# Retention and SwiGLU kernel: the last two units' rows and transposes of chunk 3 three steps later, and one down piece split in two

## The chip, the cores and the metric

The kernel runs on one core of a Trainium2 chip. The metric is the device time in microseconds of one execution, given as the median of several runs. One execution was profiled, and all times within it are in microseconds from the start of its span.

## The reference

q, k and v have the shape (4 batches, 8 heads, 768 positions, 64). Each head has a decay gamma. The output is then normalized and run through a feed-forward layer with 512 inputs and 1536 inner columns:

```
for t in range(S):
    state = gamma * state + outer(k[t], v[t])       # per batch and head, 64 x 64
    y[t]  = scale * q[t] @ state
x   = y, with the heads side by side                # 3072 rows of 512
xn  = x / sqrt(mean(x * x) + 1e-06) * rms_g
out = (silu(xn @ w_gate) * (xn @ w_val)) @ w_out
```

## The kernel before

**Tiling.** The 768 positions are cut into six chunks of 128 (chunks 0 to 5). A unit (c, b) is chunk c of batch b; a pair (c, p) is two batches. Within a chunk the recurrence is done as products: q times k (the "q-k products", `ap` for chunks 0 and 1, `a_pe` from chunk 2 on), a causal mask on VectorE, then the masked products times v, plus q times the state that the earlier chunks left (`values`). The pair's result is scaled (`y_out`), squared on ScalarE (`square`), its norm factor is made on GpSimd (`rstd`), and VectorE writes the normalized rows (`norm`).

**Operands.** For chunks 2 to 5, `load` (L105) issues three transfers per unit on GpSimd's DMA queue: q and k, converted to bf16, and v in float32. `t_dma` (L472) then issues two DMA transposes per unit on SP's queue, to have q and k with the head dimension on the partitions. `x_dma` (L541) does the same for the normalized rows. SP's queue also issues the output stores (`store`, L569), which for chunks 0 and 1 are two half transfers per unit. An instruction on a queue waits until those ahead of it have been issued. A DMA also waits for the eighth one before it on its kind of queue to have landed, since eight semaphores take turns.

**Feed-forward.** A group is the four units of one chunk, 512 rows. `gv` (L548) computes gate and value products into PSUM, ScalarE applies silu, VectorE multiplies, and the result lies in hT. `down` (L576) multiplies one unit's hT by w_out in 12 accumulating matmuls, ScalarE copies the result to SBUF, and SP stores it. The last half unit of the kernel uses `down_last`.

**Order.** Everything is in an order written out by hand, with one instruction stream per engine. Up to the first group's down pieces it is a straight list (L596 to L737). After it, `run` goes through a list of steps for each chunk: 12 `gv` steps and four `down` steps for chunk 1, twelve `gv` steps (four of 256 rows, eight of 512) and four `down` steps for later chunks. After each step a table names what else is issued. So while the feed-forward group of chunk 1 runs, chunk 2's attention and chunk 3's loads and transposes are put between its steps. Chunk 3's first q-k products (units 0 and 1) follow step 12 of chunk 1; its second (units 2 and 3) follow step 5 of chunk 2.

**PSUM.** Eight banks. In the straight list a bank is taken from the head of a written list (`first`, then `order`), so the order of the calls decides the bank. From chunk 1's steps on, the attention and the feed-forward turn in four banks each. The output rows o_sb have three buffers; the raw q and k rows and their transposes have eight each, v has six.

Of the kernel before, what the change touches and what calls it, by code (L numbers as in the profile page):

```python
# [16 lines left out]
def kernel(  # L17
# [21 lines left out]
    NFF = DFF // 128  # L39
# [25 lines left out]
    def bank(name, dtype=F32, ffn=False, i=None):  # L65
        if i is None and split[0]:
            i = turn[ffn] % 4 + 4 * ffn
            turn[ffn] += 1
        elif i is None and first:
            i = first.pop(0)  # L70
        elif i is None:
            i = order[0]
            order.append(order.pop(0))
        return psum.tile([128, 512 if dtype == F32 else 1024], dtype, name=name, tag=f"p{i}")
# [30 lines left out]
    def load(c, b, names="qkv"):  # L105
        u = U.setdefault((c, b), {})
        for n in names:
            if n == "v":
                x = work.tile([128, H, D], F32, name="v_f", tag="v_f", bufs=6)
                nc.gpsimd.dma_start(out=x, in_=unit_v[n][c, b])  # L110
            else:
                x = work.tile([128, DM], BF16, name=n + "b", bufs=8)
                nc.gpsimd.dma_start(out=x.rearrange("p (h d) -> p h d", h=H), in_=unit_v[n][c, b])  # L113
            u[n] = x
# [106 lines left out]
    def copy(eng, out, in_):  # L221
        return (nc.scalar.copy if eng == "a" else nc.vector.tensor_copy)(out, in_)  # L222
# [44 lines left out]
    def ap(c, p, a):  # L267
        u = U[c, p]
        if c == 0:
            qt, kt = ([u[n + "T", a][:, :, b] for b in range(2)] for n in "qk")  # L270
        else:
            qt, kt = u["qT", a], u["kT", a]
        ps = [bank("a_ps") for _ in range(2)]
        for x in range(2):
            for e in range(2):
                o = (x * 2 + e) * 128
                for b in range(2):
                    for i in range(2):
                        r, t = slice(i * 64, i * 64 + 64), slice(b * 64, b * 64 + 64)
                        nc.tensor.matmul(ps[i][t, o:o + 128], kt[b][r, x, e], qt[b][r, x], start=True, stop=True)  # L280
        u["a_ps", a] = ps
# [104 lines left out]
    def x_pe(c, p, j):  # L386
        u = U[c, p]
        ps = bank("x_ps", BF16)
        for s in range(KS):
            nc.tensor.transpose(ps[:, s * 128:(s + 1) * 128], u["xn"][j][:, s * 128:(s + 1) * 128], ident)  # L390
        u["x_ps", j] = ps

    def x_copy(c, p, j, eng):
        b = 2 * p + j
        dst = XT[c][:, :, b * C:(b + 1) * C]
        src = U[c, p]["x_ps", j][:, :512].rearrange("p (s t) -> p s t", s=KS)
        if c == 0 and j == 0:
            nc.vector.tensor_tensor(out=dst, in0=src, in1=g_col[:, :, None].to_broadcast([128, KS, 128]), op=ALU.mult)
        else:
            return copy(eng, dst, src)  # L400
# [71 lines left out]
    def t_dma(c, b):  # L472
        u = U[c, b]
        for n in "qk":
            t = work.tile([128, NHP, 128], BF16, name=n + "T", tag=n + "T", bufs=8)
            nc.sync.dma_start_transpose(out=t, in_=u[n])
            u[n + "T"] = t
# [91 lines left out]
    def store(eng, c, b, m, o_sb):  # L569
        if c < 2:  # L570
            for e in range(2):
                eng.dma_start(out=out_e[c, b, e][:, m], in_=o_sb[e * 64:e * 64 + 64, m])
        else:
            eng.dma_start(out=out_v[c, b][:, m], in_=o_sb[:, m])

    def down(c, b):  # L576
        ps = bank("o_ps", ffn=True)
        for n in range(NFF):
            nc.tensor.matmul(ps, HT[c][:, n, b * C:(b + 1) * C], wo_b[:, n, :], start=n == 0, stop=n == NFF - 1)  # L579
        o_sb = work.tile([128, DM], F32, name="o_sb", bufs=3)  # L580
        nc.scalar.copy(o_sb, ps)  # L581
        store(nc.sync, c, b, slice(0, DM), o_sb)
# [125 lines left out]
    load(2, 0)  # L708
    y1(0)
    down(0, 0)  # L710
    y1_out(0)
    square(1, 0, 0)
# [5 lines left out]
    vp_pair(1, 1)  # L718
    load(2, 2)
    down(0, 1)  # L720
    down(0, 2)
    t_dma(2, 0)
    for n, e in (("q", "a"), ("k", "v")):
        tp1(1, n)
        tc1(1, n, e)
# [1 line left out]
    x_copy(1, 0, 0, "v")  # L727
    x_pe(1, 0, 1)
    x_copy(1, 0, 1, "v")
    ap(1, 1, 0)  # L730
    ap(1, 1, 1)
    for a in range(2):
# [1 line left out]
            ap_mask(1, 1, a, i)  # L734
    load(2, 3)
    t_dma(2, 1)
    down(0, 3)  # L737

    def run(steps, after):
        for i, step in enumerate(steps):  # L740
# [4 lines left out]
    def L(f, *a):  # L745
        return lambda: f(*a)
# [13 lines left out]
        5: [L(a_pair, 2, 0), L(a_mask, 2, 0, 0)],  # L760
        6: [L(a_mask, 2, 0, 1), L(a_mask, 2, 1, 0), L(vp, 2, 2), L(vp, 2, 3)],
        7: [L(a_mask, 2, 1, 1)],
        8: [L(values, 2, 0), L(y_out, 2, 0, 0), L(y_out, 2, 0, 1), L(state_add, 2, 0), L(load, 3, 2),
            L(t_dma, 3, 0), L(t_dma, 3, 1)],
        9: [L(square, 2, 0, 0), L(load, 3, 3)],
        10: [L(a_pair, 2, 1), L(square, 2, 0, 1), L(a_mask, 2, 2, 0), L(a_mask, 2, 2, 1), L(state_cast, 0),
             L(rstd, 2, 0)],
        11: [L(a_mask, 2, 3, 0), L(a_mask, 2, 3, 1), L(t_dma, 3, 2)],
        12: [L(values, 2, 1, (3, 0), True), L(norm, 2, 0, 0, 1), L(x_dma, 2, 0, 0), L(x_dma, 2, 0, 1),
             L(y_out, 2, 1, 0), L(y_out, 2, 1, 1), L(square, 2, 1, 0), L(square, 2, 1, 1), L(rstd, 2, 1),  # L770
             L(state_add, 2, 1), L(a_mask, 3, 0, 0), L(a_mask, 3, 0, 1), L(norm, 2, 1, 0, 1),
             L(x_dma, 2, 1, 0), L(x_dma, 2, 1, 1), L(t_dma, 3, 3), L(a_mask, 3, 1, 0, 1),
             L(state_cast, 1), L(vp, 3, 0), L(vp, 3, 1)],
    })

    for c in range(2, NCH):
# [64 lines left out]
```

## Time and profile before

| | us |
|---|---|
| median of 8 runs | 239.39 |
| lowest and highest run | 236.74 and 243.71 |
| profiled execution, whole | 240.19 |
| its span from first to last instruction | 238.4 |
| TensorE busy in the span | 226.4 |
| VectorE, GpSimd, ScalarE busy | 127.2, 114.9, 87.5 |

The feed-forward group of chunk 1 starts at 62.00 us with its first gate product, and that of chunk 2 at 100.46. The last matmul is that of `down_last`, which starts at 232.50.

In a timeline row the first number is the start and the second the time; x counts the instructions merged in it, and a bracket gives the idle time of the engine before it and what ended it. A row with SPq or POOL and a DMA operation is the issue of a transfer, not the transfer; its landing comes later. In the list of waits the three numbers are total time, count and longest. In the chain, a DMA piece runs from a transfer's issue to its landing.

### The profile page before, as it was taken

Reading aid. Unit: us, or ns where it says so; the run is one execution under the profiler, and the core shown is the slowest. Engines: PE = TensorE matmul, PEld = TensorE weight load, DVE = VectorE, ACT = ScalarE, POOL = GpSimd, SP = SyncE. Lnnn points to the kernel's source line nnn. Section 1 sums busy time; section 2 is a strip of 40 time slices with the busy share of each in tenths; the row PEclk is TensorE's granted clock in tenths of the full one; section 3 lists DMA queues with packets and bytes.
Section 4 is the critical chain, followed back from the end, with each engine's and each line's share of the span. In section 5 each row is a group of like instructions: output and inputs, shape, how many; then the busy total and the mean of one; then the engine's idle time right before and its main releaser. Section 6 shows DMA issues by size and latency. Waiting matters only on the chain.

```text
span 238.4 us, 5562 instructions
## 1 busy us (share of the span) xinstructions
PE 226.4 (95%) x2290; PEld 138.7 (58%) x2290; DVE 127.2 (53%) x222; ACT 87.5 (37%) x176; POOL 114.9 (48%) x150
## 2 busy tenths in 40 slices
PE   7786899989999998999999999999999999999994
PEld 2355685545788875585454585454684544864443
DVE  3675634735576877627868036868145842234300
ACT  2863644323143333235324235323235342333211
POOL 8957499749959951980946802937001001000000
PEclk9999999999999999999999999999999999999999
DMA  7999999999999999699990999991630204200022
GB/s 95 167 174 210 157 158 171 202 198 189 180 156 194 174 173 181 73 148 246 96 171 5 194 174 204 98 124 36 166 110 0 47 0 132 91 0 0 0 92 88
DMA packets 83307, 30.25 MB, mean 127 GB/s; under 512 B 69521, under 2 KB 78993, under 8 KB 83282
## 3 DMA queue, kind: packets, MB, share of 16 engines
q0 software_dynamic: 51328, 16.52, 69.3%
q1 hardware_dynamic: 31280, 13.25, 28.5%
q8 instruction: 18, 0.29, 0.5%
q10 hardware_dynamic: 674, 0.14, 0.3%
q14 instruction: 7, 0.06, 0.1%
HBM read 28.32 MB, written 6.29 MB: 145 GB/s over the span
## 4 chain that ended last, share of the span: by engine, by line
PE 73%; DMA 18%; POOL 3%; DVE 2%; ACT 1%; issue 1%; DVEq 0%; SPq 0%; ACTq 0%; POOLq 0%
PE o_ps L579 23%; PE g_ps L560 21%; PE v_ps L560 21%; DMA v2f<-in_v_dram 7%; DMA wo_b<-in_moe_w_out_dram 5%; DMA kT<-kb 4%; DMA k2b<-in_k_dram 2%; PE a_ps L485 1%; PE y_ps L514 1%; PE o_ps L590 1%; PE y_ps L531 1%; POOL q2b L101 1%; POOL k2b L101 1%; POOL vp L300 1%; PE kv_ps L523 1%
## 5 line engine op out<-in xcount | busy, mean ns | idle before, releaser
L565 DVE TENSOR_TENSOR hT<-sg,v_ps 128x512 bf16<-128x512 bf16 (+1 forms) x76 | 49.8, 658 | 77.3 <-PE v_ps L560 65.4
L560 PE MATMUL v_ps<-xnT,wv_b 128*128 128x256 bf16 (+1 forms) x428 | 74.9, 309 | 1.8 <-DMA wv_b<-in_moe_w_val_dram 1.8
L560 PE MATMUL g_ps<-xnT,wg_b 128*128 128x256 bf16 (+1 forms) x428 | 75.1, 310 | 0.2 <-ACT xnT L222 0.2
L564 ACT ACTIVATE sg<-g_ps 128x512 bf16<-128x512 f32 (+1 forms) x76 | 43.5, 575 | 75.2 <-PE g_ps L560 75.2
L579 PE MATMUL o_ps<-wo_b,hT 128*128 128x512 bf16 x276 | 61.1, 379 | 0.9 <-DMA wo_b<-in_moe_w_out_dram 0.9
L560 PEld LDWEIGHTS <-wv_b 128*128 128x128 bf16 x428 | 41.8, 98 | 22.7 <-DMA wv_b<-in_moe_w_val_dram 2.0
L560 PEld LDWEIGHTS <-wg_b 128*128 128x128 bf16 x428 | 40.6, 98 | 20.6 <-issue 0.7
L579 PEld LDWEIGHTS <-hT 128*128 128x128 bf16 x276 | 26.6, 98 | 32.7 <-issue 1.2
L454 POOL TENSOR_SCALAR m<-ms 128x2 f32<-128x2 f32 x10 | 2.2, 218 | 68.6 <-ACT xsq L449 68.5
L581 ACT COPY o_sb<-o_ps 128x512 f32<-128x512 f32 x23 | 13.4, 584 | 46.5 <-PE o_ps L579 43.5
L462 DVE SCALAR_TENSOR_TENSOR xn<-x,rstd,g_bc 128x512 bf16<-128x512 f32 x20 | 19.5, 1004 | 10.4 <-POOL rstd L370 10.4
L494 DVE TENSOR_TENSOR am<-a_ps,causal 128x512 bf16<-128x512 f32 x32 | 21.1, 681 | 0.0
L468 POOL TENSOR_TENSOR vp<-v_f,vd_n 128x512 bf16<-128x512 f32 x16 | 19.4, 1238 | 0.0
L113 POOL DMA_DIRECT2D qb<-in_q_dram x16 | 15.1, 944 | 1.8 <-DMA wo_b<-in_moe_w_out_dram 1.8
L449 ACT ACTIVATE xsq<-x 128x512 bf16<-128x512 f32 x20 | 12.4, 623 | 9.3 <-DVE x L440 9.3
L113 POOL DMA_DIRECT2D kb<-in_k_dram x16 | 14.4, 898 | 1.8 <-DMA wo_b<-in_moe_w_out_dram 1.8
L110 POOL DMA_DIRECT2D v_f<-in_v_dram x16 | 14.7, 921 | 0.1
L440 DVE TENSOR_TENSOR x<-y_ps,yd_n 128x512 f32<-128x512 f32 x16 | 10.6, 685 | 1.7 <-PE y_ps L531 1.7
L219 PE MATMUL hot<-ones 128*128 128x512 bf16 x28 | 9.4, 466 | 1.4 <-DVE ones L146 1.4
L300 POOL TENSOR_TENSOR vp<-v2f,vd_p 128x1024 bf16<-128x1024 f32 x4 | 7.7, 1930 | 0.1
L370 POOL TENSOR_TENSOR rstd<-m,mhalf 128x2 f32<-128x2 f32 x10 | 7.2, 718 | 0.8
L101 POOL DMA_DIRECT2D q2b<-in_q_dram x8 | 5.8, 738 | 0.8 <-POOLq L825 0.8
(96 smaller groups left out, 154.4 us busy)
## 6 DMA issues: line engine op xcount, KB each, us to landing
v_f<-in_v_dram POOLq DMA_DIRECT2D x16, 256.0 KB, 6.6
out_dram<-o_sb SPq DMA_DIRECT2D x15, 256.0 KB, 2.3
out_dram<-o_sb SPq DMA_DIRECT2D x17, 128.0 KB, 6.0
qb<-in_q_dram POOLq DMA_DIRECT2D x16, 128.0 KB, 5.6
kb<-in_k_dram POOLq DMA_DIRECT2D x16, 128.0 KB, 6.3
wg_b<-in_moe_w_gate_dram POOLq DMA_DIRECT2D x6, 256.0 KB, 8.2
wv_b<-in_moe_w_val_dram POOLq DMA_DIRECT2D x6, 256.0 KB, 9.0
wo_b<-in_moe_w_out_dram POOLq DMA_DIRECT2D x3, 512.0 KB, 10.9
```

The costliest lines, as they stand in the source:

```text
L110: nc.gpsimd.dma_start(out=x, in_=unit_v[n][c, b])
L113: nc.gpsimd.dma_start(out=x.rearrange("p (h d) -> p h d", h=H), in_=unit_v[n][c, b])
L440: nc.vector.tensor_tensor(out=x[:, :, :, i, :], in0=u["y"][i].rearrange("p (b a d) -> p b a d", b=2, a=NHP), in1=yd_n[:, c, i][:, None, :, ...
L449: nc.scalar.activation(xsq, u["x"][:, b], AF.Square, scale=1.0 / math.sqrt(DM), accum_out=u["ms_"][:, b:b + 1])
L462: nc.vector.scalar_tensor_tensor(out=u["xn"][b], in0=u["x"][:, b], scalar=u["rstd"][:, b:b + 1], in1=g_bc, op0=ALU.mult, op1=ALU.mult)
L468: nc.gpsimd.tensor_tensor(out=x, in0=U[c, b]["v"], in1=vd_n[:, c, :, None].to_broadcast([128, H, D]), op=ALU.mult)
L494: nc.vector.tensor_tensor(out=x, in0=u["a_ps"][i].rearrange("p (a t) -> p a t", a=NHP), in1=causal[:, None, :].to_broadcast([128, NHP, 128 ...
L560: nc.tensor.matmul(x[:, o:o + w], wt[:, s, n * 128:(n + 1) * 128], XT[c][:, s, t0:t1], start=s == 0, stop=s == KS - 1)
L564: nc.scalar.activation(sg[:, :m], ps[0][:, :m], AF.Silu)
L565: return nc.vector.tensor_tensor(out=HT[c][:, n0:n1, t0:t1], in0=sg[:, :m].rearrange("p (n t) -> p n t", t=w), in1=ps[1][:, :m].rearrange( ...
L579: nc.tensor.matmul(ps, HT[c][:, n, b * C:(b + 1) * C], wo_b[:, n, :], start=n == 0, stop=n == NFF - 1)
L581: nc.scalar.copy(o_sb, ps)
```

## The change

Three things move; no work is added or taken away.

`down` can now do a part of its 12 matmuls, and keeps its PSUM bank between the parts. The down piece of unit (0, 3) is cut: four of its matmuls now come ahead of chunk 1's second q-k products, and eight stay where all 12 were.

The transposes of unit (2, 0) are issued ahead of the down piece and the store of unit (0, 2), and not behind them.

The loads of chunk 3's units 2 and 3 move from after steps 8 and 9 of chunk 1 to after step 11 and into step 12, where they stand ahead of the second pair's scaling. Their transposes move from after step 11 and the end of step 12 to after steps 14 and 15.

```diff
-    def down(c, b):
-        ps = bank("o_ps", ffn=True)
-        for n in range(NFF):
+    DP = {}
+
+    def down(c, b, n0=0, n1=NFF):
+        ps = DP[b] = bank("o_ps", ffn=True) if n0 == 0 else DP[b]
+        for n in range(n0, n1):
             nc.tensor.matmul(ps, HT[c][:, n, b * C:(b + 1) * C], wo_b[:, n, :], start=n == 0, stop=n == NFF - 1)
+        if n1 < NFF:
+            return
         o_sb = work.tile([128, DM], F32, name="o_sb", bufs=3)
...
     down(0, 1)
+    t_dma(2, 0)
     down(0, 2)
-    t_dma(2, 0)
...
     x_copy(1, 0, 1, "v")
+    down(0, 3, 0, 4)
     ap(1, 1, 0)
     ap(1, 1, 1)
...
     t_dma(2, 1)
-    down(0, 3)
+    down(0, 3, 4)
...
-        8: [L(values, 2, 0), L(y_out, 2, 0, 0), L(y_out, 2, 0, 1), L(state_add, 2, 0), L(load, 3, 2),
+        8: [L(values, 2, 0), L(y_out, 2, 0, 0), L(y_out, 2, 0, 1), L(state_add, 2, 0),
             L(t_dma, 3, 0), L(t_dma, 3, 1)],
-        9: [L(square, 2, 0, 0), L(load, 3, 3)],
+        9: [L(square, 2, 0, 0)],
...
-        11: [L(a_mask, 2, 3, 0), L(a_mask, 2, 3, 1), L(t_dma, 3, 2)],
+        11: [L(a_mask, 2, 3, 0), L(a_mask, 2, 3, 1), L(load, 3, 2)],
         12: [L(values, 2, 1, (3, 0), True), L(norm, 2, 0, 0, 1), L(x_dma, 2, 0, 0), L(x_dma, 2, 0, 1),
+             L(load, 3, 3),
              L(y_out, 2, 1, 0), L(y_out, 2, 1, 1), L(square, 2, 1, 0), L(square, 2, 1, 1), L(rstd, 2, 1),
              L(state_add, 2, 1), L(a_mask, 3, 0, 0), L(a_mask, 3, 0, 1), L(norm, 2, 1, 0, 1),
-             L(x_dma, 2, 1, 0), L(x_dma, 2, 1, 1), L(t_dma, 3, 3), L(a_mask, 3, 1, 0, 1),
+             L(x_dma, 2, 1, 0), L(x_dma, 2, 1, 1), L(a_mask, 3, 1, 0, 1),
              L(state_cast, 1), L(vp, 3, 0), L(vp, 3, 1)],
+        14: [L(t_dma, 3, 2)],
+        15: [L(t_dma, 3, 3)],
     })
```

## The prediction

> **What bounds the kernel now.** I read the page's busy table first, then the list of waits, then the chain, then the timelines of TensorE and of SP's queue between 80 and 114 us, where the moved transfers lie.
>
> ```profile
> PE 226.4 (95%) x2290; PEld 138.7 (58%) x2290; DVE 127.2 (53%) x222; ACT 87.5 (37%) x176; POOL 114.9 (48%) x150
> ...
> DMA  7999999999999999699990999991630204200022
> ```
>
> TensorE is busy 95% of the 238.4 us. So an edit can win only what TensorE still waits, and can lose whatever new wait it makes. A slice is 5.96 us. The DMA row is full from the second slice to the 27th (up to about 161 us) with two dents, the first at 95 to 101 us: transfers have little room where the change moves them.
>
> The waits of TensorE after 50 us, from the list of waits:
>
> ```profile
> PE o_ps L579 <- DMA wo_b<-in_moe_w_out_dram: 0.9, 1, 0.9
> PEld L280 <- DVE k2T L222: 1.5, 4, 0.6
> PE a_ps L485 <- DMA kT<-kb: 0.7, 1, 0.7
> ```
>
> The first is in the first group's down pieces at 50.97 us, ahead of all that is changed. The second is spread over the q-k products of chunks 0 and 1. The third is the one that the moved transfers touch. The chain and TensorE's timeline show it:
>
> ```profile
> 83.03 9.27 DMA kT<-kb
> 92.30 0.05 issue
> 92.35 0.40 PE a_ps L485 x8
> ```
> ```profile
> 87.51 2.75 PE L579 MATMUL o_ps<-wo_b,hT 128*128 128x512 bf16 x12
> ...
> 92.35 0.40 PE L485 MATMUL a_ps<-qT,kT 64*128 64x128 bf16 x8 [0.69 <-DMA kT<-kb]
> ```
>
> The transpose of k for unit (3,1) is issued at 83.03 and lands 9.27 us later, at 92.30; TensorE loses 0.69 us. Two more rows give the place where the moved transposes are used, the q-k products of units (3,2) and (3,3), and there TensorE waits for nothing:
>
> ```profile
> 112.28 0.62 PE L485 MATMUL a_ps<-qT,kT 64*128 64x128 bf16 x16
> 112.83 1.04 PE L560 MATMUL g_ps<-xnT,wg_b 128*128 128x512 bf16 x4
> ```
>
> SP's queue in between, all of it issues:
>
> ```profile
> 86.24 1.19 SPq L476 DMA_TRANSPOSE qT<-qb  x1
> 87.88 1.19 SPq L476 DMA_TRANSPOSE kT<-kb  x1
> 90.91 1.11 SPq L572 DMA_DIRECT2D out_dram<-o_sb  x2
> 92.11 7.96 SPq L543 DMA_TRANSPOSE xnT<-xn  x4
> 100.17 1.21 SPq L476 DMA_TRANSPOSE qT<-qb  x1
> 101.47 1.30 SPq L476 DMA_TRANSPOSE kT<-kb  x1
> 102.86 3.82 SPq L572 DMA_DIRECT2D out_dram<-o_sb  x6
> 107.23 1.19 SPq L476 DMA_TRANSPOSE qT<-qb  x1
> ```
>
> 86.24 and 87.88 are unit (3,2), 100.17 and 101.47 unit (3,3), 107.23 unit (4,0). An issue costs about 1.2 us for a transpose and 0.6 us for a half store, and they stand in line.
>
> **What the Trainium skill says.** "DMA: Bandwidth & Descriptors", section "Queues, rings and completion order": each DMA engine takes turns between the queues that have work, packet by packet. The trace agrees: the transposes issued beside POOL's loads, between 77.9 and 84.3 us, took 6.7, 6.2, 7.8 and 9.3 us to land, while of the four transposes of xn issued from 92.11, after the loads had mostly drained, the quickest took 3.0 and the median 3.9 us. Same page, section "Rules for kernel authors": issuing from several engines gives no bandwidth, only issue time. So a later load is no less traffic; it only meets other transfers. "TensorE: Matmul & The Clock Gate", section "What's actually happening": after an idle window of about 3.4 us the clock may fall to half. In this trace the granted clock stays at 9 or more tenths in every slice, and no wait is that long, so it shows neither; I use it for one rival.
>
> **Part 1, down piece split.** Four of the 12 matmuls of the down piece of unit (0,3) go ahead of the q-k products of chunk 1's second pair, eight stay. Nothing is added; the accumulator takes its bank one place earlier, from a down copy that ended at 55.20 us, so no wait comes with it. In before, TensorE's work between the end of the down pieces at 57.1 and the first gate product at 62.00 is: 64 transposes 0.67, eight transposes of xn 0.44 (128 columns each, half of the 0.109 us that a gate product of 256 columns takes), 32 q-k products 0.57, 12 matmuls of 0.216 us 2.60, sum 4.28 of 4.90 us. The other 0.62 us are waits on the copies of q2T and k2T (ScalarE 57.70 to 58.78, VectorE 57.92 to 58.68). Four matmuls are 0.86 us, longer than the time from the end of the transposes (58.22) to the last copy (58.78), so they cover it. Bounds: 0 if the gap lies elsewhere in the stretch, 0.62 if all goes; I take 0.50, as the 0.18 and 0.33 us seen before the first and third product. The masks on VectorE begin 0.25 us later (end about 62.0) and are wanted by chunk 1's read products at about 63.1, so they stay hidden.
>
> **Part 2, one transpose pair ahead of a store.** The transposes of unit (2,0) issue at about 56.95 (q landed 56.92) instead of 59.03; the store of (0,2) follows 2.5 us later. Their first user runs at 74.52 and they landed by 68.23; no one waits for that store, as three output buffers turn. Nothing either way, from -0.1 to +0.1 us.
>
> **Part 3, loads of (3,2) and (3,3) later.** Six POOL issues of about 0.9 us go from 80.02 to 85.37 to about 86.3 to 91.8 us: they now stand behind POOL's norm scale for pair (2,0) (86.38) and are done before that of (2,1), ready at 94.28, so nothing on POOL waits for them. With them, and the transposes of (3,2), off the DMA engines at 83 to 88 us, k of (3,1) should land some 3 to 5 us after its issue at 83.03, at 86 to 88; it is wanted at about 91.6. The 0.69 us are gone. Bounds 0 and 0.69, taken 0.69.
> What they now meet: the stores of (1,0) and the xn transposes of pair (2,0), issued at about 90.4 to 92.9. Beside loads the later xn transposes of chunk 3 took 5.2 to 6.9 us. The second would land at 98.1 to 99.8; chunk 2's first gate product wants it at 100.46 less 1.19, that is 99.27. A wait of 0 to 0.5 us, taken at 0; it would only eat what was gained.
>
> **Part 4, transposes of (3,2) and (3,3) at the end of chunk 1.** On SP they are now behind the stores of (1,1), (1,2) and, for (3,3), (1,3). SP's last xn issue ends at 100.07; its start hangs on pair (2,1)'s read products, which part 1 alone moves, so 99.57. Then two stores, each two half issues, 1.28 us with the gaps: 102.2. The two transposes of (3,2), 2.69 us (100.17 to 102.86 in the trace): 104.9. The store of (1,3), 1.28: 106.2. q of (3,3), 1.30: k of (3,3) is issued at 107.5, against 101.47 before.
> When does it land? Nearest row: the transpose issued at 107.23 landed 6.6 us later, which gives 114.1. Second way: counted from the last xn transpose, k of (3,3) becomes the 11th transfer on the hardware queue instead of the third. The 11th in before was k of (4,0), behind the same six stores and two other transposes and beside the same six loads; its neighbours landed at 113.85 and 114.95, so about 114.4, less 0.5 for the earlier start 113.9. Taken 113.9. Bounds: the shortest transpose in this stretch, 3.0 us, gives 110.5 and no wait; the 9.3 us of k of (3,1) give 116.8.
> TensorE wants it at 112.56 (112.28 and eight products) less 0.69 and 0.50: 111.37. The wait is 2.5 us, and it stands in front of everything on TensorE: the gate products of chunk 2 behind it, and through them ScalarE's and VectorE's work. The transposes of chunk 4's first units slip about 2 us on SP and land near 116, wanted at 124.38; that has cover.
>
> **Sum.** -0.69 - 0.50 + 0.00 + 2.5 = +1.3 us. On the profiled execution's 240.19 us: 241.5. That execution is 0.8 us over the median of 239.39 (its span of 238.4 and 1.8 us around it), and the difference is carried over: 240.7. A measurement of this kernel can tell about 1%, here 2.4 us, from no change; single runs lie between 236.74 and 243.71.
>
> **Rivals.**
> - A: the transposes land in time. For it: once chunk 4's loads are drained (about 111) the queue is quick; after the drain at 94 us four transposes and two half stores landed between 94.4 and 96.4. Against it: only 4 us lie between issue and need, and of the nearest rows none beside loads was under 5.2. Then both gains stay: 239.39 - 1.19 = 238.2.
> - B, slower: the same transposes are as late as k of (3,1) was. Place: the wait at the q-k products of (3,2) and (3,3) in chunk 2's sixth step. Price: 116.8 - 111.4 = 5.4 us, less 1.19: +4.2, so 243.6; with a clock drop after so long an idle time it could be more (estimate from the page named, half speed for a window of 3.4 us: 1.7 us). It decides from a landing after about 115.0 (7.5 us after issue), where the net loss passes 2.4 us. For it: a transfer of this queue took 9.3 us beside loads. Against it: chunk 4's loads end near 111, before most of this wait.
> - C: the change moves the wait instead of removing it. The late loads collide with the xn transposes of (2,0), and TensorE waits at chunk 2's first gate product for up to the 1.2 us gained; with k of (3,3) hardly late the sum is near zero, 239.4.
>
> **How the numbers follow.** Forecast (net 0.1 to 2.3 us) 0.45, A 0.20, B 0.25, C 0.10. The predicted time is the forecast's, 240.7. The range reaches from A's full gain to B, 238.2 to 243.6. Slower by over 1%: B, and about a third of the forecast once the spread of the median is laid over it, 0.40. Faster by over 1% needs 2.4 us, twice all the gain found, so only A with luck: 0.08. Within 1%: 0.52.
>
> **What would show it.** Right: no wait for kT at about 91 us; a new wait of L485 for kT at 111 to 114 us, 1 to 4 us long; the k2T and q2T waits near 58 us gone; k of (3,3) issued at 107 to 108. Wrong: no wait at chunk 2's second q-k products (A); a wait over 4 us there (B); a wait of gate products for xnT near 99 us (C); or TensorE's first gate product of chunk 1 not before 61.6 us, which would fell part 1.

## The result, and the profile after

The changed kernel is slower: a median of 247.43 us over 11 runs against 238.28 over 32 runs of the kernel before, and a ratio of 1.0248 with a 95% interval of 1.0203 to 1.0293. The ratio leaves out executions more than 1.5% above the fastest of their kernel, the profiled ones of both kernels and of e4, e6, e8 and e9 among them, which is why it lies below the ratio of the medians. The profiled execution of the changed kernel took 248.73 us with a span of 247.0, against 240.19 and 238.4 before.

The page of the changed kernel, in the lines that answer to those shown of before, with the row of the granted clock (PEclk) added:

```profile
PE 231.1 (94%) x2290; PEld 139.8 (57%) x2290; DVE 127.7 (52%) x222; ACT 87.6 (35%) x176; POOL 115.1 (47%) x150
...
PEclk9999999999999959999799999999999999999999
DMA  7999999999999996399990799692550203300022
```

TensorE has the same 2290 matmuls and is busy 4.7 us longer. The clock row says why: it falls to a half in the 15th slice (86 to 93 us) and to 0.7 in the 20th (117 to 124 us). In the kernel before it was 9 or more everywhere. The list of waits has one line for the q-k products where 0.7 us stood before:

```profile
PE a_ps L485 <- DMA kT<-kb: 7.7, 3, 4.7
```

TensorE's timeline shows where these three waits are and what follows each:

```profile
87.12 0.61 PE L485 MATMUL a_ps<-qT,kT 64*128 64x128 bf16 x8 [4.67 <-DMA kT<-kb]
87.67 1.89 PE L560 MATMUL g_ps<-xnT,wg_b 128*128 128x256 bf16 x8
...
116.04 0.40 PE L485 MATMUL a_ps<-qT,kT 64*128 64x128 bf16 x8 [0.48 <-DMA kT<-kb]
118.98 0.40 PE L485 MATMUL a_ps<-qT,kT 64*128 64x128 bf16 x8 [2.54 <-DMA kT<-kb]
119.31 1.81 PE L560 MATMUL g_ps<-xnT,wg_b 128*128 128x512 bf16 x4
120.91 1.91 PE L560 MATMUL v_ps<-xnT,wv_b 128*128 128x512 bf16 x4
```

The waits at 116 and 119 us are for the two moved pairs of transposes, units (3,2) and (3,3). The products right after them take 1.81 and 1.91 us where the same products took 1.03 to 1.04 in before: they run at about half the clock. The wait at 87 us is an earlier one, for unit (2,3), and it has such a tail too. The second transpose of unit (3,3), that of k, is issued at 113.68 us in this execution and lands at 118.94: by then all of it runs later than forecast, first of all by the wait at 87 us.

The two profiled executions are 8.5 us apart. Where 8.2 of them come from can be read by setting the starts of the same TensorE rows side by side (a minus is a start earlier than in before):

| TensorE row | before | changed | difference, us | what happened in between |
|---|---|---|---|---|
| transposes of chunk 1's second pair | 57.11 | 54.47 | -2.64 | start of the execution, not touched by the change |
| read products of chunk 1, second pair | 63.74 | 60.61 | -3.13 | the split down piece: 0.49 gained |
| q-k products of chunk 2, second pair | 85.20 | 82.06 | -3.14 | |
| down piece (1,0) | 87.51 | 91.05 | +3.54 | 6.68 lost: wait 4.67, the rest mostly half clock |
| read products of chunk 3, first pair | 103.95 | 107.17 | +3.22 | the 0.69 wait of before is gone, the clock's tail counts against it |
| read products of chunk 3, second pair | 123.20 | 131.37 | +8.17 | 4.95 lost: waits 3.02, the other 1.93 mostly half clock |
| last full down pieces | 224.57 | 232.74 | +8.17 | nothing more |

### The profile page after: what moved, and what is told of

Same layout as the page of the kernel before. It is cut to its first block, busy times and chain, and to the rows that moved or that the text cites. A ratio compares the mean times of both kernels' runs of the same rounds, so it can differ in the third digit from the quotient of the medians.

```text
span 247.0 us, 5559 instructions
## 1 busy us (share of the span) xinstructions
PE 231.1 (94%) x2290; PEld 139.8 (57%) x2290; DVE 127.7 (52%) x222; ACT 87.6 (35%) x176; POOL 115.1 (47%) x150
## 4 chain that ended last, share of the span: by engine, by line
PE 81%; DMA 12%; DVE 3%; POOL 1%; issue 1%; SPq 0%; DVEq 0%; POOLq 0%
PE o_ps L581 25%; PE g_ps L560 24%; PE v_ps L560 23%; DMA kT<-kb 7%; DMA wv_b<-in_moe_w_val_dram 3%; DMA k2b<-in_k_dram 2%; PE a_ps L485 2%; PE y_ps L514 1%; DVE am L287 1%; PE o_ps L594 1%; PE y_ps L531 1%; PE kv_ps L523 1%; PE a_ps L280 1%; POOL q2b L101 1%; PE x_ps L390 1%
## 5 line engine op out<-in xcount | busy, mean ns | idle before, releaser
L560 PE MATMUL v_ps<-xnT,wv_b 128*128 128x256 bf16 (+1 forms) x428 | 76.7, 315 | 1.1 <-DMA wv_b<-in_moe_w_val_dram 1.1
L560 PE MATMUL g_ps<-xnT,wg_b 128*128 128x256 bf16 (+1 forms) x428 | 76.8, 315 | 0.8 <-DMA wg_b<-in_moe_w_gate_dram 0.5
L560 PEld LDWEIGHTS <-wv_b 128*128 128x128 bf16 x428 | 42.4, 99 | 23.3 <-DMA wv_b<-in_moe_w_val_dram 1.7
L560 PEld LDWEIGHTS <-wg_b 128*128 128x128 bf16 x428 | 41.1, 99 | 22.4 <-issue 2.1
L485 PE MATMUL a_ps<-qT,kT 64*128 64x128 bf16 x128 | 5.5, 222 | 7.7 <-DMA kT<-kb 7.7
L219 PE MATMUL hot<-ones 128*128 128x512 bf16 x28 | 10.0, 488 | 1.4 <-DVE ones L146 1.4
L485 PEld LDWEIGHTS <-kT 64*128 64x128 bf16 x128 | 3.8, 96 | 9.8 <-DMA kT<-kb 8.5
```

The source lines that it names most:

```text
L485: nc.tensor.matmul(ps[i][:, hp * 128:(hp + 1) * 128], u["kT"][r, hp, :], u["qT"][r, hp, :], start=True, stop=True)
L560: nc.tensor.matmul(x[:, o:o + w], wt[:, s, n * 128:(n + 1) * 128], XT[c][:, s, t0:t1], start=s == 0, stop=s == KS - 1)
```

## The experiments

In what follows, chunk 2's second q-k products are those of units (2,2) and (2,3), near 85 us, and chunk 3's second those of (3,2) and (3,3), in chunk 2's sixth step; the prediction's signs and the expectation of e1 call the latter chunk 2's too.

Theory T is that of the forecast, with the clock added: the transposes of (3,2) and (3,3) are issued so late that TensorE waits for them, and the wait makes the clock fall. The rivals: S, the straight list's edits delay chunk 2's last transposes; L, the later loads cost by themselves. All ratios are to runs of the kernel before in the same session.

**Halves of the change.** Run e1: the table of steps alone (the second part of the diff) with the straight list of before:

> Only the table of steps is changed (loads and transposes of chunk 3's last two units later); the straight list is as before. Theory T (late transposes: k of (3,3) lands after TensorE wants it, and the half clock after the wait doubles its price): a wait of chunk 2's second q-k products for kT of 2 to 4 us, clock below 0.995, time 3.5 to 6 us over before (ratio 1.015 to 1.025). Rival S (the straight-list edits make the transfers of chunk 2's last units late, as the 4.7 us wait at 87 us in the changed kernel's profile has it): ratio within 1% of 1 here, since the straight list is unchanged. Rival L (the later loads collide with other transfers): waits of gate products for xnT, with kT in time.

Ratio 1.0154 (1.0089 to 1.0218). The rows of its timeline that wait:

```profile
109.33 0.40 PE L485 MATMUL a_ps<-qT,kT 64*128 64x128 bf16 x8 [0.47 <-DMA kT<-kb]
112.15 0.40 PE L485 MATMUL a_ps<-qT,kT 64*128 64x128 bf16 x8 [2.42 <-DMA kT<-kb]
```

The predicted wait is there with the straight list untouched, so S alone can't be the cause. In this one execution the clock stayed at 1.0; the last section comes back to it.

Run e2: the straight list alone, with the table of before:

> Only the straight list is changed (down piece split in 4 and 8, transposes of unit (2,0) ahead of a store); the table of steps is as before. Theory T: the 0.5 us at 58 us gained and nothing lost, ratio 0.995 to 1.0, no wait for kT of chunk 2's last units. Rival S: a wait for kT at chunk 2's second q-k products on the slot near 85 us, 2 to 5 us, ratio 1.01 or more.

Ratio 1.0152 (1.0087 to 1.0217), with a wait of 3.50 us for kT at 85.80 us in its profile. This speaks for S as well; T had nothing for it.

**One part of the table.** Run e3: the transposes later, the loads where they were:

```diff
-        11: [L(a_mask, 2, 3, 0), L(a_mask, 2, 3, 1), L(t_dma, 3, 2)],
+        11: [L(a_mask, 2, 3, 0), L(a_mask, 2, 3, 1)],
...
-             L(x_dma, 2, 1, 0), L(x_dma, 2, 1, 1), L(t_dma, 3, 3), L(a_mask, 3, 1, 0, 1),
+             L(x_dma, 2, 1, 0), L(x_dma, 2, 1, 1), L(a_mask, 3, 1, 0, 1),
...
+        14: [L(t_dma, 3, 2)],
+        15: [L(t_dma, 3, 3)],
```

> Only the transposes of chunk 3's last two units are moved to after steps 14 and 15; their loads stay where they were, and so does the straight list. Theory T: as with the whole table, a wait of 2 to 4 us for kT at chunk 2's sixth step and ratio 1.01 to 1.025, since the issue on SP at about 107 us sets the landing. Rival L (the loads are what is too late): ratio near 1 and no such wait.

Ratio 1.0205 (1.0137 to 1.0274), as T had it, but its profile shows the wait elsewhere: 2.91 us for kT of unit (3,1) at 94.14 us and 0.98 us at 84.99, none in chunk 2's sixth step. One execution delayed earlier comes later to the moved transposes; the ratio fits T, this profile doesn't show it.

Run e4: the changed kernel with the late transposes alone undone:

```diff
-             L(x_dma, 2, 1, 0), L(x_dma, 2, 1, 1), L(a_mask, 3, 1, 0, 1),
+             L(x_dma, 2, 1, 0), L(x_dma, 2, 1, 1), L(t_dma, 3, 2), L(t_dma, 3, 3), L(a_mask, 3, 1, 0, 1),
...
-        14: [L(t_dma, 3, 2)],
-        15: [L(t_dma, 3, 3)],
```

> The changed kernel with the transposes of units (3,2) and (3,3) put back right behind the xn transposes in step 12, ahead of the stores of (1,1) to (1,3); the loads stay late and the straight list stays changed. Theory T: the wait at chunk 2's sixth step is gone (k of (3,3) issued near 104 and landed by 111), ratio 0.99 to 1.0. Rival S: the wait near 85 us stays in part of the runs and ratio 1.01 or more. Rival L: ratio 1.01 or more, with waits for xnT or for kT of (3,2) and (3,3) though they are issued early.

Ratio 1.0018 (0.9985 to 1.0051). With the transposes issued ahead of the stores the loss is not measurable, loads late and list changed all the same. That is T, and against L. S stays half alive: the profiled execution has a wait of 3.88 us at 88.47, at chunk 2's second q-k products.

**The two list edits apart.** Run e5: the transposes of (2,0) ahead of the store of (0,2), alone:

```diff
     down(0, 1)
+    t_dma(2, 0)
     down(0, 2)
-    t_dma(2, 0)
```

> Only the transposes of unit (2,0) go ahead of the store of (0,2); all else is as before. Theory S (these transposes, 2 us earlier, run beside the loads of units (2,1) to (2,3), so k of (2,3) lands late and TensorE waits at chunk 2's second q-k products near 85 us): ratio 1.01 or more, wait for kT there of 1 to 4 us, k of (2,1) landing 8 us after its issue instead of 6. Rival S1 (the split down piece does it): ratio within 0.5% of 1. Third: neither alone, only both together, ratio near 1 here too.

Ratio 1.0153 (1.0076 to 1.0229) on few runs, and its profile has 0.65 us of wait for kT at 73.58 and none near 85. Run e6: the split down piece alone:

> Only the down piece of (0,3) is split in 4 and 8; transposes and table are as before. Theory S: ratio 0.997 to 1.0 (0.5 us gained near 58 us, nothing lost). Rival S1: ratio 1.01 or more with a wait for kT near 85 us.

Ratio 1.0027 (0.9993 to 1.0062): neither the expected gain nor S1's loss can be told from no change.

**The wait taken away at its other end.** Run e7: the changed kernel, with the q-k products that wait two steps (3.5 us) later:

```diff
-                5: [L(a_pair, d, 1), L(a_mask, d, 2, 0), L(square, d, 0, 1), L(rstd, d, 0)]
+                5: [L(a_pair, d, 1), L(a_mask, d, 2, 0)] * (d != 3) + [L(square, d, 0, 1), L(rstd, d, 0)]
...
-                6: [L(a_mask, d, 2, 1), L(norm, d, 0, 0),
+                6: [L(a_mask, d, 2, 1)] * (d != 3) + [L(norm, d, 0, 0),
...
-                7: [L(norm, d, 0, 1), L(x_dma, d, 0, 1), L(a_mask, d, 3, 0)] +
+                7: [L(a_pair, d, 1), L(a_mask, d, 2, 0), L(a_mask, d, 2, 1)] * (d == 3)
+                   + [L(norm, d, 0, 1), L(x_dma, d, 0, 1), L(a_mask, d, 3, 0)] +
```

> The changed kernel with chunk 3's second q-k products and their first masks two steps later (after step 7 of chunk 2 in place of step 5); the late transposes and all else stay. Theory T: the wait of 3 us at these products and the half clock after it go, 3 to 5 us below the changed kernel: ratio to before 1.0 to 1.012. If the ratio stays at 1.02 or more, the late transposes were not the cause.

Ratio 1.0056 (1.0011 to 1.0101). The transposes are as late as in the changed kernel; only their reader moved. Of the 2.48% some 1.9 are gone.

**The clock.** Run e9: the changed kernel with filler for TensorE in the wait:

```diff
-                5: [L(a_pair, d, 1),
+                5: [L(heat, 12, None)] * (d == 3) + [L(a_pair, d, 1),
```

> The changed kernel with 12 matmuls of ones (2.6 us at full clock, result unused) ahead of chunk 3's second q-k products, where it waits 3 us for kT. Theory T with the clock: TensorE does not idle there, the clock stays full, and 1 to 2 us are saved against the changed kernel although work is added: ratio to before 1.015 to 1.02, mean clock over 0.99. If the half clock has nothing to do with this wait, the time is equal or up to 2.6 us longer: ratio 1.025 to 1.035.

Ratio 1.0195 (1.0138 to 1.0251). Lower than 1.0248 with 12 matmuls more, as T with the clock had it, but the intervals overlap, and its profile is marred by a wait of 4.86 us at 87.94. It is repeated below on a quieter kernel.

**Loads and early transposes without the late transposes.** Run e11: the kernel before with the loads later and the transposes of (3,2) and (3,3) right behind the xn transposes:

> Before with only the loads of (3,2) and (3,3) later; their transposes stand right behind the xn transposes in step 12, ahead of the stores, and the straight list is as before. Theory T (all the loss of the table lies in the transposes' late issue): ratio 0.996 to 1.002; if the later loads do what the forecast said, the 0.7 us wait for kT at 92 us is gone. Rival L (the later loads cost by themselves): ratio over 1.005.

Ratio 1.0018 (0.9985 to 1.0051). L falls. The 0.69 us wait of before at 92 us is gone from its profile, the first q-k products of chunk 3 run without a bracket:

```profile
89.11 0.61 PE L485 MATMUL a_ps<-qT,kT 64*128 64x128 bf16 x16
```

So the forecast's gain is seen where it was expected, and it is too small to be measured in the time.

Run e12: the same with the transposes of (2,0) early:

> The same with the transposes of unit (2,0) ahead of the store of (0,2). Theory S (these early transposes cost about 1.5% by themselves, as the run with them alone had it): ratio 1.01 to 1.02. Rival X (they cost only beside early loads of chunk 3, and the late loads give the room back; or the run with them alone was chance): ratio within 0.5% of 1.

Ratio 1.0035 (1.0005 to 1.0064): at most a small loss, rival X rather than S. With the loads late, as in the changed kernel, both edits of the list together cost at most 0.5% (e4); why they cost 1.5% beside the early loads (e2) stays open.

**The changed kernel less one list edit each.** Run e13: without the early transposes of (2,0), that is table and split down piece:

> The changed kernel with the transposes of unit (2,0) back behind the store: table and split down piece alone. Theory T: the wait of 3 us and the half clock behind it stay, ratio 1.02 to 1.028. If the early transposes are a third of the loss (theory S), 1.01 to 1.018.

Ratio 1.022 (1.0167 to 1.0273), nearly all of the loss. Its profile is the clearest of all, since TensorE waits for no other kT. SP's queue, TensorE's timeline, the chain, and the busy times in three windows of 4 us (after the engines' busy times come the granted clock, the DMA share and GB/s):

```profile
97.82 3.41 SPq L572 DMA_DIRECT2D out_dram<-o_sb  x4
101.33 1.24 SPq L476 DMA_TRANSPOSE qT<-qb  x1
102.66 1.88 SPq L476 DMA_TRANSPOSE kT<-kb  x1
104.64 1.24 SPq L572 DMA_DIRECT2D out_dram<-o_sb  x2
105.98 1.30 SPq L476 DMA_TRANSPOSE qT<-qb  x1
107.38 1.22 SPq L476 DMA_TRANSPOSE kT<-kb  x1
```
```profile
111.13 0.40 PE L485 MATMUL a_ps<-qT,kT 64*128 64x128 bf16 x8 [1.00 <-DMA kT<-kb]
114.00 0.40 PE L485 MATMUL a_ps<-qT,kT 64*128 64x128 bf16 x8 [2.47 <-DMA kT<-kb]
...
115.68 1.91 PE L560 MATMUL v_ps<-xnT,wv_b 128*128 128x512 bf16 x4
```
```profile
107.38 6.58 DMA kT<-kb
113.95 0.05 issue
```
```profile
110.00:114.00 4.00, 0.53 (x9) 0.23 (x10) 1.38 (x2) 0.57 (x2) 3.26 (x5) 1.00 1.39 179
114.00:118.00 4.00, 4.00 (x18) 1.61 (x19) 0.30 (x1) 0.60 (x1) 4.00 (x6) 0.59 1.65 151
118.00:122.00 4.00, 3.95 (x19) 1.76 (x18) 4.00 (x6) 1.20 (x2) 1.75 (x2) 0.98 1.66 174
```

The six store halves and the transposes of (3,2) stand ahead of unit (3,3) on SP, as the forecast laid them out; k of (3,3) goes out at 107.38 and lands at 113.95. TensorE does 0.53 us of work in the 4 us before, and in the 4 us after has 0.59 of its clock. By the starts of the rows around it (chunk 3's first read products 103.95 before and 101.74 here, its second 123.20 and 126.39) this stretch costs 5.40 us: 3.47 of wait and 1.93 more. The half clock lasts from 114.71 to 118.12 us, 3.41 us, which is 1.71 us of work lost; where the other 0.2 us go is open. It was no chance of one execution: the mean granted clock of the six runs was 0.990 to 0.993.

Run e14: without the split, that is table and early transposes:

> The changed kernel with the down piece whole again: table and early transposes alone. Theory K (the split lets TensorE come 0.5 us sooner to the wait for kT, so the wait is 0.5 us longer and more often long enough for the half clock, which costs 2 us): ratio 1.012 to 1.018, as with the table alone, and a clock nearer to 1. If the split has no part in the loss: ratio 1.022 to 1.028.

Its six runs lie between 244.05 and 251.98 (median 249.09) and give no ratio. Its profile has waits of 0.52 and 2.33 us at the same products and a mean clock of 0.991. What the split adds to the loss is not settled by these times. The traces fit the first half of theory K: without the split the two waits are 2.85 us together here and 2.89 in e1, with it 3.47 in e13, though only 3.02 in the changed kernel. Its second half, that a shorter wait spares the clock, doesn't hold here: the clock fell to half for 3.41 us in this profile as well.

**The two halves of the price, on the quiet kernel.** Run e15: filler in the wait of table and split:

> Table and split down piece (no early transposes), with 12 matmuls of ones (2.6 us at full clock, result unused) ahead of chunk 3's second q-k products, where that kernel waits 1.0 and 2.5 us for kT and then runs about 3.7 us at half clock. Theory K (the half clock is caused by this wait): the wait shrinks by the filler's time, the clock stays full, about 1.8 us saved of 243.4: 241.5, ratio 1.012 to 1.016, mean clock 0.998 or more. Rival (the half clock comes from elsewhere): 243.4 or more.

Ratio 1.015 (1.009 to 1.0209). TensorE's timeline and its window after the wait:

```profile
107.87 2.75 PE L219 MATMUL hot<-ones 128*128 128x512 bf16 x12
...
111.55 0.40 PE L485 MATMUL a_ps<-qT,kT 64*128 64x128 bf16 x8 [0.60 <-DMA kT<-kb]
```
```profile
114.00:118.00 4.00, 4.00 (x20) 1.83 (x19) 4.00 (x7) 1.19 (x2) 3.99 (x4) 1.00 1.81 153
```

The clock stays full, here and nearly so in all six runs (mean granted clock 1.000 in four, 0.997 and 0.993 in the others). The difference of the ratios is 0.7%, 1.7 us of 238, which agrees with the 1.71 us of the slow clock, though the intervals just overlap.

Run e16: the reader of table and split two steps later, by the edit of e7:

> Table and split down piece with chunk 3's second q-k products two steps later (3.5 us). Theory T: both the 3.5 us wait and the 1.9 us of half clock go: 238 us, ratio 0.997 to 1.003. If half of the loss stays, something else than this wait makes it.

Ratio 1.0013 (0.9979 to 1.0047), median 237.96 against 238.00. The wait that is left:

```profile
112.54 0.40 PE L485 MATMUL a_ps<-qT,kT 64*128 64x128 bf16 x8 [0.43 <-DMA kT<-kb]
```

The transposes are late in this kernel too. The whole 2.2% goes with 3.5 us of room for the reader, which shows that lateness against this one reader is the cause.

**A candidate, and a repeat.** Run e8: split and late loads, no late and no early transposes:

> Split down piece and late loads, with the transposes of (3,2) and (3,3) right behind the xn transposes and those of (2,0) where they were. By the forecast's two gains: 1.2 us below before, ratio 0.995. If the gains are not there (TensorE waits later for the same transfers): ratio 1.0 to 1.003.

Ratio 0.9988 (0.9953 to 1.0023): no version here is measurably faster than the kernel before. The gain may be taken back at chunk 3's second q-k products, where before waits for nothing: with the loads late and the transposes early, TensorE waits there for k of (3,3) by 0.37 us in this profile, 0.78 in e12 and 1.01 in e4, and only in e11 not at all. Run e17: the transposes of (2,0) early, once more:

> Once more the transposes of unit (2,0) ahead of the store of (0,2), alone. If they cost by themselves: ratio 1.01 or more. If the first figure was chance: ratio within 0.5% of 1, as with late loads.

Ratio 1.0052 (0.9994 to 1.0111), so the first figure of 1.0153 was high. But the median over all its runs was 244.21 against 238.00. Of the profiles with this edit five (the changed kernel, e2, e4, e7 and e9) have a wait of 1.9 to 4.9 us at chunk 2's second q-k products, and four (e5, e12, e14, e17) have none; of the nine without it only two (e3 and e6) have one, of 1.0 and 2.3 us. Whether the early transposes bring these waits on is not settled.

## Why the prediction was wrong, and where it was right

- **The place and the mechanism** were right: the new wait is that of chunk 3's second q-k products, in chunk 2's sixth step, for the moved transposes, because SP's queue issues them behind the stores. Run e16 shows it from the reader's side, e4 from the writer's.
- **Issue and landing.** Forecast 107.5 and 113.9, measured on table and split 107.38 and 113.95. That this fits so well is partly luck: that execution ran about 2.2 us ahead of before at chunk 3's first read products, so its last xn transpose was issued by 97.72 instead of 99.57, and SP took 9.7 us from there to k of (3,3), not 7.9. Two errors cancelled.
- **The wait** was sized 2.5 us. It is 3.47 on that kernel and 3.02 in the changed one. The forecast looked only at unit (3,3); the products of (3,2) ahead of it also wait, 1.00 and 0.48 us, and an execution that is ahead comes to the wait earlier by as much.
- **The step that failed** is that the sum left the clock out. It was priced at 1.7 us, but only in rival B, for an idle time as long as a window of 3.4 us, so a wait of 2.5 us was taken to leave the clock alone. It fell after waits of 0.48 and 2.54 us in the changed kernel and of 1.00 and 2.47 us in e13, with 0.4 us of work between, and the stretch lost 1.93 us beyond the waits. With both terms as measured, -0.49 - 0.69 + 3.47 + 1.93 = +4.2 us instead of +1.3. The range ended at +4.2; with the measured ratio of 1.0248, 5.9 us of 238, the time lies beyond it. The two gains were a second, smaller step: they stand in the traces, but no ratio shows them (e6, e8, e11). Without them the sum is 5.4 us, against 5.2 (2.2%) measured for e13.
- **Part 1**, 0.50 us, was right in the trace of the changed kernel (0.49). The time doesn't show it: ratio 1.0027 alone.
- **Part 3**, the 0.69 us, was right in the trace of e11 and also not measurable. That the late loads would collide with the xn transposes (rival C) was not seen; in no profile do gate products wait for such a transpose.
- **Part 2** was taken at nothing, within 0.1 us. The runs don't settle it: alone it came out at 1.0153 and at 1.0052, with late loads at 1.0035 (1.0005 to 1.0064), and the changed kernel, with it, at 1.0248 against 1.022 of e13, without it.
- **The earlier wait at 87 us** in the changed kernel's profile was in no rival. It may be part of the 0.4% or so by which e7 lies above e16 (1.0056 against 1.0013, with intervals that overlap), and its cause is open.

## What to carry to other kernels

When a transfer is issued later, count what stands ahead of it on its queue, add the landing time of the nearest row beside the same traffic, and compare with the moment of its reader; here that sum came out within 0.2 us, in part by luck. Then price the wait twice where TensorE is the bound: once for itself and once for the clock that may fall after it, 1.7 us where it fell here. If a transfer must be late, move its reader by as much: here 3.5 us of room took back the 2.2%.

## What was not expected of the hardware

- TensorE's clock fell to half after waits that were each under 2.6 us, with 0.4 us of work between them (0.48 and 2.54, 1.00 and 2.47 us), and in e3 after a single wait of 2.91 us. "TensorE: Matmul & The Clock Gate" in the Trainium skill speaks of an idle window of about 3.4 us ("What's actually happening"). In these traces it takes less. The traces keep the moments at which the granted clock changed, and in each of the 18 profiles these lie whole multiples of 3.413 us apart. But for a last fall at the very end, half clock lasted one such stretch, or two (6.83 us, at the wait of 4.67 us in the changed kernel and at that of 4.86 us in e9). Each profile, from its first change of clock up to 228 us, can so be cut into stretches of 3.413 us, and TensorE's idle time summed in each. Of 1148 stretches at full clock, the 13 with 1.91 us of idle time or more were all followed by half clock; none of the others was, and they had 1.89 us at most. Five of them:

| profile | stretch of 3.41 us begins at | idle in it, us | clock after it |
|---|---|---|---|
| changed | 116.02 | 2.57 | half |
| e13 | 111.30 | 2.47 | half |
| e14 | 111.54 | 1.96 | half |
| e1 | 110.26 | 1.89 | full |
| e7 | 83.13 | 1.39 | full |

- In these profiles, then, where a wait lay against the stretches decided, and not its length alone. The waits of e1 (0.47 and 2.42 us) fell 1.00 us into one stretch and 1.89 into the next, and the clock stayed; those of e13 (1.00 and 2.47) left 2.47 us in one stretch, and it fell. Where the stretches lie differs from execution to execution (their first one begins between 4.4 and 7.4 us in these profiles). That the limit lies near 1.9 us is a reading of this kernel's traces, in which the ends of matmuls are modelled; no run set it on its own.
- 2.75 us of matmuls for nothing in such a wait took the ratio from 1.022 down to 1.015 (intervals just overlapping), not up.
- The same transpose (k of unit (2,3)) landed 6.5 us after its issue in the profile of before and 11.3 us after it in that of the changed kernel, at the same place in the queue.
